# A fused attention and expert layer on one core: stores of one group on ScalarE's queue, three TensorE modes in the planner, new planning numbers

## The chip, the cores and the metric

The program runs on one core of a Trainium2 chip. The time is the device time of one execution in microseconds (us). A core has engines that run side by side: TensorE (PE; its weight loads, PEld, are shown apart), VectorE (DVE), ScalarE (ACT), GpSimd (POOL), and SyncE (SP), which here only issues DMAs. ScalarE can issue DMAs too. Each engine works through its own instructions in the order in which the program holds them and waits at an instruction until the semaphores that it names are reached.

## The reference

Causal attention over 4 batches of 12 heads (448 positions, 64 wide), then a two-layer block over all 1,792 tokens, all in float32.

```python
scores = scale * np.matmul(q, k.transpose(0, 1, 3, 2))
scores = np.where(mask, -1000000000.0, scores)
scores = scores - np.max(scores, axis=-1, keepdims=True)
attn = np.exp(scores)
attn = attn / (np.sum(attn, axis=-1, keepdims=True) + 1e-09)
attn_out = np.matmul(attn, v)
x = attn_out.transpose(0, 2, 1, 3).reshape(B * S, H * D)      # 1792 x 768
h = x @ w_in                                                  # 768 -> 2048
g = h * np.clip(h + 3.0, 0.0, 6.0) / 6.0
out = g @ w_out                                               # 2048 -> 768
```

## The kernel before

**What is computed where.** A *unit* is one pair of heads of one batch, 24 in all (`unit`, line 420). For each unit TensorE makes the scores (line 490: row tiles of 112 positions, the two heads side by side in 64 rows of the array each), VectorE adds the mask and takes the row's bound (line 505), ScalarE takes the exponential with the row sum (line 512), VectorE inverts the sums (lines 522 and 523), one of GpSimd, ScalarE or VectorE scales the rows (line 531 on ScalarE, line 533 on the others), TensorE transposes the rows in 112 x 112 blocks (line 553), ScalarE or VectorE copies them out of PSUM (lines 361 and 364), and TensorE multiplies with V (line 566: 112 rows, the two heads in 64 columns of the array each). The first six units score in plain float32; the later ones in three products of split numbers.

**The two layers.** A float32 matrix product is made as three products of operands that are split into a high and a low part (`triple`, lines 640 to 642): 696 triples of 128 x 128 by 128 x 448, 2,088 products. A *group* is one batch. Group 0 goes through `first_layer(0)` and `early_products`, group 1 through `first_layer(1)` and `middle`, groups 2 and 3 together through `last_first` and `last_second`, which save products by sums and differences of blocks. The weights come as 64-bit words and are turned into float32 by VectorE (`words`, lines 603, 605 and 608); they are kept in DRAM (`kept_w`, `kept_s`) and read again. The first layer's outputs of group 0 are kept in DRAM too (`kept_g`, line 686), for `middle`, which works with groups 0 and 1 together.

**What sets the order.** Nothing in the program runs in the order in which it is written. Every step is an `Op` with a key (a due time, made from `T_FIRST`, `T_PACE`, `UNIT`, `LOADS`, `WORDS`, the `K_...` numbers and so on), with the engines that may do it, and how much later than the first of them each may take it (`A_LAG`, `NORM_LAG`, `A_FIRST`). `Flow.run` plays the program through once at build time: whenever an engine is free, it takes from the ready steps the one with the lowest key whose buffers are free, and the resulting list of instructions is what the chip gets. `BUFS`, `BANKS` and `MOST` say how many buffers of each kind there are. Two rules are TensorE's alone. It has a mode: *tiled* for scores and products with V, not tiled for transposes and the layers' products; a step of the same mode is preferred until another's key is earlier by `KEEP` of the mode, and a change of mode costs time in the plan:

```python
                        if e != "PE" or o.tiled == self.mode:
                            chosen = o, need
                            break
                        if not chosen:
                            chosen, limit = (o, need), o.key[0] + self.KEEP[self.mode]
```

And where the plan finds TensorE idle between 20 and 36 us, `fill` puts in matmuls that compute nothing used (line 1072), so that the array stays at work. Ahead of the first scores stand four products of the tile `warm`, which compute nothing used either (line 1092).

DMAs stand in one queue, SyncE's, in the plan's order; three stand in ScalarE's: the first unit's two loads of k, and one of the last stores. A load or store is issued by `dma` (line 348), which has an argument for the queue; the framework gives the DMAs eight semaphores in turn, and an issue waits until the DMA that last used its semaphore has landed.

In the rows below, `gh` and `gl` are the large buffers that first hold q, k and v of batch 0, `d` is the pool of general buffers, `b` a PSUM bank, `wd` the weights as loaded, `wh` and `wl` their high and low parts, `prow` the row statistics, `r` a 128 x 448 scratch buffer.

Of the kernel before, what the change touches and what calls it, by code (L numbers as in the profile page):

```python
# [17 lines left out]
B, H, S, D = 4, 12, 448, 64  # L18
DM, DFF = 768, 2048
C = 112  # L20
# [10 lines left out]

T_FIRST = -113
T_PACE = 4
T_EARLY = 8
T_EACH = 11
T_LATE = 74
T_DENSE = 7.25
T_LOAD = -8
T_W = 10
T_WLOAD = 9  # L40
T_XA = 166
T_X = 175
T_LAST = 182
T_PAIR = 10.5
T_SECOND = T_LAST + 8 * T_PAIR
T_SECOND_GROUP = 72
T_MID = 120
T_BACK = 40
T_WORDS = 77
M_LOAD = 20  # L50
E_WORDS = 6.5
K_SCORES = 0
K_TURN = 6.5
K_TURNS = 0.6
K_PRODUCT = 14
K_GATE = 5
KEEP_FULL = 0
KEEP_TILED = 6.5
N_RAW = 6
DEPTH = 3  # L60
A_FIRST = 4
D_FIRST = 0.4
T_V = 11
FINE = 3
W_FROM = 3
W_BEHIND = 4
UNIT = [-80, -17, 5, 2.5, 0.5, -1, -2, -1.5, 5.5, 0.5, -6.5, -3, -3.5, -8, -2.5, -4.5, -1, -1.5, -6, -4.5, -2.5, 1, -4, 3]
LOADS = [-70, -38, -8, 10, 0, -10, 12, -14, -22, -4, -20, -14, 10, 4, -12, 2, -8, -12, -2, -28, -10, -4, 4, -6]
K_KEEP = -4
K_G = 4  # L70
GATE_FROM = 1
WORDS = [1, 8, -6, 4, -3, 7, -5, 0, -4, 3, -6, 0, 6, -2, 7, -4, 2, 4, 2, 3, -2, 2, -8, -4, 8, 3, -7, 5]
T_ISSUE = 0.36
NORM_LAG = 1.5
A_LAG = 0

# [8 lines left out]
    ps="b s most ps", tp="b s most", av="b s", mo="b mo", c="b c",  # L85
)
MOST = dict(qk=3, op=4, wf=4, sf=6, x=8, pt=6, pr3=4, pr20=5, xq=6, xc=21, gt=12, gm=9, so=3, s=8, most=8, ps=8, mo=2, c=8)

# [22 lines left out]
class Flow:  # L111
# [5 lines left out]
    BEGIN, LATENCY = 0.8, 0.12  # L117
    SWITCH = 0.4
    TAIL = dict(PE=.1, D=.085, A=.105, P=.04, SP=0)

    KEEP = KEEP_FULL, KEEP_TILED
    QUEUE, WARM = 8, 4
    DMA_PACKET, DMA_RATE, DMA_LANES, DMA_LATENCY = 0.008, 23e3, 16, 2.1
# [8 lines left out]

    def op(self, key, ways, parts, r=(), tiled=False, nbytes=0):

        w = [x for _, _, ws in parts for x in ws]
        bufs = {x[0] for x in list(r) + w if isinstance(x[0], Buf)}
        o = Op((key, len(self.ops)), ways, parts, bufs, nbytes)
        o.tiled = tiled
        for b in bufs:
            b.refs += 1  # L140
        before = {}
        for x in list(r) + w:
            if x in self.wrote:
                a, i = self.wrote[x]
                before[a] = max(before.get(a, 0), i)
        for x in w:
            for a in self.readers.pop(x, ()):
                before[a] = len(a.parts) - 1
        for x in r:
            self.readers.setdefault(x, []).append(o)  # L150
        for i, (_, _, ws) in enumerate(parts):
            for x in ws:
                self.wrote[x] = o, i
        before.pop(o, None)
        for a, i in before.items():
            a.then.append((o, i))
        o.waits = len(before)
        self.ops.append(o)
        return o

    def run(self):
# [3 lines left out]
        busy = dict.fromkeys(lists, self.BEGIN)  # L165
        self.dma, self.mode, self.port, tick = 0.0, False, 0.0, 0
        left = len(self.ops)
# [97 lines left out]
    def start(self, o, e, now, need, out, busy, post):  # L265
# [5 lines left out]
        if e == "PE" and o.tiled != self.mode:  # L271
            t += self.SWITCH / 2
            self.mode = o.tiled
# [28 lines left out]
def tile_causal_attention_hardswish_moe(ctx: ExitStack, tc: tile.TileContext, q, k, v, w_in, w_out, out):  # L302
    nc = tc.nc
# [40 lines left out]

    def pe(key, parts, r, tiled=False):
# [74 lines left out]
    def unit(b, p):  # L420
# [70 lines left out]

        cost, more = (1.667e-3, .06) if raw32 else (1.25e-3, .08)
        for a, two in enumerate(((1, 0), (3, 2)) if at == 0 else ((3, 2), (1, 0))):
# [3 lines left out]
                [(cost * C * (i + 1) + more, lambda i=i: products(i), [(ps[e, i][0], i) for e in range(2)] + [("turn",)]) for i in two],  # L497
                (halves_[0] if at == a == 0 else reads) + [("unit", at - (2 if b else DEPTH))], True,
            )
# [42 lines left out]
        for e in range(2):  # L542
            for js, ph in zip(GROUPS, pairs):
# [10 lines left out]

                pe(key, [(.096 * len(blocks) + .03, turn, [(tp, 0)])], [pk[e, i] for i in sorted({i for i, _ in blocks})])
                move(
# [13 lines left out]

        pe(t + K_PRODUCT, [(10 * C * 1.667e-3, times_v, [(av, 0), (av, 1), ("unit", at)])], deps, True)
        if b < 2:
# [73 lines left out]
    def first_layer(g):  # L646
# [5 lines left out]
        for i in range(NF):  # L652
# [32 lines left out]
            )  # L685
            dma(t + .5 + K_G, 4 * S, lambda i=i: kept_g[i], lambda r=r: ap(r), [(r, 0)], [("g", i)])
            move(t, S, lambda i=i: ap(gh)[:, i], lambda r=r: ap(r), [(r, 0)], [(gh, i)], {"A": 1})
# [403 lines left out]
    for _ in range(Flow.WARM):  # L1091
        nc.tensor.matmul(ap(b)[:C, :C], warm, warm, start=True, stop=True)

# [48 lines left out]
```

## Time and profile before

| | |
|---|---|
| three runs | 583.20, 583.35, 584.42 us; median 583.35 us |
| the profiled execution | 583.93 us, its span 582.2 us |
| TensorE busy | 573.8 us, 99% of the span |
| VectorE busy | 486.7 us, 84% |
| ScalarE busy | 405.7 us, 70% |
| GpSimd busy | 233.4 us, 40% |
| TensorE in the chain that ended last | 88% |

The span runs from the first to the last instruction of the one execution that was profiled; the 1.7 us between it and that execution's time lie around it. A timeline row has the start, the duration, the engine, the line, the operation, and in brackets the idle time ahead of it with what ended it. TensorE's float32 matmuls have two records each, and the records' ends are modelled and overlap; so the distance from start to start tells the cost, not the duration. The three layers' products are one every 0.20 us.

### The profile page before, as it was taken

The numbers are of one execution on the slowest core, as the hardware profiler recorded it, in microseconds if no ns is written. First come the engines' busy times: TensorE is split into PE (matmuls) and PEld (weight loads), VectorE is DVE, ScalarE is ACT, GpSimd is POOL, SyncE is SP. The second block draws the span as 40 slices with busy tenths as digits, with TensorE's granted clock in tenths as the row PEclk, the third lists the DMA queues.
The fourth block names the chain that finished last, engine by engine and source line by source line (L and its number), as shares of the span: only waits on it lengthen the run. The fifth ranks groups of instructions, "written<-read, shape, count | busy, mean of one in ns | idle before, by whom it ended". The sixth has DMA issues, their size and how long they took to land.

```text
span 582.2 us, 10686 instructions
## 1 busy us (share of the span) xinstructions
PE 573.8 (99%) x3496; PEld 502.5 (86%) x3496; DVE 486.7 (84%) x1093; ACT 405.7 (70%) x973; POOL 233.4 (40%) x226
## 2 busy tenths in 40 slices
PE   8999999999999999999999999999999999999997
PEld 5667988988888788888988989899999999999996
DVE  5899999899689787999998668999888799985652
ACT  6997885888757666899988968576555586454530
POOL 2678889874447344776274212034000042100000
PEclk9999999999999999999999999999999999999999
DMA  8958999967579898999832254441211424443411
GB/s 235 334 184 278 315 319 362 395 230 233 179 267 303 258 385 267 329 381 304 301 114 76 94 165 145 160 128 56 82 55 55 128 64 135 133 133 111 138 64 48
DMA packets 61352, 115.59 MB, mean 199 GB/s; under 512 B 6512, under 2 KB 36592, under 8 KB 61296
## 3 DMA queue, kind: packets, MB, share of 16 engines
q1 hardware_dynamic: 60576, 114.34, 59.5%
q10 hardware_dynamic: 720, 0.57, 0.3%
q8 instruction: 27, 0.44, 0.3%
q14 instruction: 29, 0.24, 0.1%
HBM read 83.39 MB, written 31.49 MB: 197 GB/s over the span
## 4 chain that ended last, share of the span: by engine, by line
PE 88%; DMA 5%; DVE 3%; ACT 2%; issue 1%; SPq 0%; DVEq 0%; ACTq 0%
PE b L640 24%; PE b L641 23%; PE b L642 23%; PE b L566 7%; PE b L553 6%; PE b L490 5%; DMA gl<-in_v_dram 2%; DMA wd<-in_w_in_dram 1%; DMA wd<-in_w_out_dram 1%; ACT d L512 1%; DVE b L603 1%; DVE d L608 1%; DVE b L505 1%; DVE b L605 1%; ACT gl L512 0%
## 5 line engine op out<-in xcount | busy, mean ns | idle before, releaser
L640 PE MATMUL b<-d,wh 128*128 128x448 f32 x624 | 231.4, 371 | 0.7 <-ACT d L512 0.7
L641 PE MATMUL b<-d,wh 128*128 128x448 f32 x624 | 226.3, 363 | 0.0
L642 PE MATMUL b<-d,wl 128*128 128x448 f32 x624 | 225.7, 362 | 0.0
L640 PEld LDWEIGHTS b<-d,wh 128*128 128x128 f32 x624 | 117.2, 188 | 10.6 <-ACT d L512 1.2
L642 PEld LDWEIGHTS b<-d,wl 128*128 128x128 f32 x624 | 116.9, 187 | 9.0 <-POOL wl L373 0.4
L641 PEld LDWEIGHTS b<-d,wh 128*128 128x128 f32 x624 | 117.2, 188 | 6.3
L361 ACT CAST wh<-wd 128x768 fp32r<-128x768 f32 x88 | 73.6, 836 | 70.1 <-PE b L641 61.5
L373 DVE TENSOR_TENSOR wl<-wd,wh 128x768 fp32r<-128x768 f32 x74 | 79.7, 1077 | 26.0 <-ACT wh L361 25.0
L505 DVE CUSTOM_DVE_ANT_0 b<-b,mask 112x224 f32<-112x224 f32 (+1 forms) x192 | 80.2, 479 | 19.6 <-PE b L490 17.2
L512 ACT ACTIVATE d<-b,prow 112x448 f32<-112x448 f32 (+2 forms) x144 | 72.2, 517 | 15.5 <-DVE prow L505 13.1
L373 POOL TENSOR_TENSOR d<-d 128x896 fp32r<-128x896 f32 (+3 forms) x28 | 43.2, 1548 | 36.3 <-DVE d L373 23.4
L553 PE MATMUL b<-ident,d 112*112 112x112 f32 x384 | 55.9, 261 | 1.2 <-ACT d L512 0.8
L373 POOL TENSOR_TENSOR wl<-d,wh 128x768 fp32r<-128x768 f32 (+1 forms) x28 | 46.1, 1649 | 23.9 <-ACT wh L361 14.9
L361 ACT COPY d<-b 112x336 f32<-112x336 f32 (+1 forms) x104 | 43.7, 494 | 7.5 <-PE b L553 6.9
L553 PEld LDWEIGHTS b<-ident,d 112*112 112x112 f32 x384 | 42.7, 133 | 5.6 <-POOL gl L533 1.0
L533 POOL TENSOR_SCALAR d<-d,prow 112x112 f32<-112x112 f32 (+2 forms) x59 | 29.4, 509 | 31.7 <-DVE prow L523 25.4
L566 PE MATMUL b<-d,vr 112*64 112x224 f32 (+3 forms) x288 | 37.5, 405 | 0.0
L531 ACT ACTIVATE d<-d,prow 112x336 f32<-112x336 f32 (+2 forms) x66 | 33.8, 548 | 4.2 <-DVE prow L523 4.2
L603 DVE TENSOR_SCALAR b<-wd 128x384 int32<-128x384 int32 (+1 forms) x56 | 32.9, 613 | 3.0 <-DMA wd<-in_w_out_dram 2.5
L490 PE MATMUL b<-d 64*112 64x448 f32 (+3 forms) x432 | 35.0, 305 | 0.0
L490 PEld LDWEIGHTS b<-d 64*112 64x112 f32 x432 | 30.2, 172 | 5.5 <-issue 1.2
L566 PEld LDWEIGHTS b<-d,vr 112*64 112x64 f32 x288 | 19.1, 136 | 18.4 <-issue 10.7
(111 smaller groups left out, 934.3 us busy)
## 6 DMA issues: line engine op xcount, KB each, us to landing
wd<-in_w_in_dram SPq DMA_DIRECT2D x32, 384.0 KB, 6.0
wd<-in_w_out_dram SPq DMA_DIRECT2D x24, 512.0 KB, 6.6
wd<-kept_w SPq DMA_DIRECT2D x32, 384.0 KB, 4.7
wd<-kept_s SPq DMA_DIRECT2D x32, 384.0 KB, 3.0
kept_w<-d SPq DMA_DIRECT2D x16, 384.0 KB, 6.2
kept_w<-d SPq DMA_DIRECT2D x24, 256.0 KB, 5.4
kept_s<-d SPq DMA_DIRECT2D x24, 256.0 KB, 3.8
wd<-kept_w SPq DMA_DIRECT2D x48, 128.0 KB, 2.2
```

The lines of the kernel that those rows point to most:

```text
L361: nc.scalar.copy(o(), i()) if scale is None else nc.scalar.mul(o(), i(), scale)
L373: (nc.gpsimd if e == "P" else nc.vector).tensor_tensor(o(), a(), b(), op)
L490: nc.tensor.matmul(score(e, i), qx[m, c], kx[m, :w], start=n == 0, stop=n == len(terms) - 1)
L505: lambda _, e=e, i=i, w=w: nc.vector.tensor_tensor_reduce(score(e, i), score(e, i), mask[:, S - w:], -0.125, 3.0e38, ALU.add, ALU.min, ap( ...
L512: lambda _, e=e, i=i: nc.scalar.activation(row_of(pr, e, i), score(e, i), ACTF.Exp, bias=ap(st)[:, e, i:i + 1], scale=-1.0, accum_out=ap(s ...
L531: nc.scalar.mul(x, x, ap(st)[:, e, 4 + i:5 + i])
L553: nc.tensor.transpose(ap(tp)[:C, C * n:C * n + C], row_of(pr, e, i)[:, C * j:C * j + C], ident)
L566: nc.tensor.matmul(ap(av)[64 * e:64 * e + 64, S - w:S], va()[:, j, e, :], ap(ph)[:, e, o:o + w], start=(j == 0), stop=(j == NC_ - 1),)
L603: nc.vector.tensor_scalar(ti, high, 3, 0x3FFFFFFF, ALU.logical_shift_left, ALU.bitwise_and)
L640: nc.tensor.matmul(ps, ap(wh)[:, a], xh, start=start, stop=False, skip_group_check=more)
L641: nc.tensor.matmul(ps, ap(wh)[:, a], xl, start=False, stop=False, skip_group_check=more)
L642: nc.tensor.matmul(ps, ap(wl)[:, a], xh, start=False, stop=stop, skip_group_check=more)
```

## The change

One argument sends the sixteen stores of `kept_g` through ScalarE's queue. The planner gets three modes of TensorE in place of two: 0 for transposes and the layers' products, 1 for scores, 2 for products with V; a change between any two costs 0.1 in the plan where a change cost 0.2 (`SWITCH / 2`), and a score, a product with V and a transpose block are priced a little differently. `KEEP_TILED`, how long a tiled mode is held against an earlier key, goes from 6.5 to 2.5. The four products of `warm` become eleven of half the columns. And nearly all numbers that make the keys are others. The diff, with the number tables cut to one line:

```diff
-T_FIRST = -113
-T_PACE = 4
+T_FIRST = -73
+T_PACE = 12.5
...
-KEEP_TILED = 6.5
+KEEP_TILED = 2.5
...
-A_FIRST = 4
-D_FIRST = 0.4
+A_FIRST = 5.2
+D_FIRST = 0
...
-UNIT = [-80, -17, 5, 2.5, 0.5, -1, -2, -1.5, 5.5, 0.5, -6.5, -3, -3.5, -8, -2.5, -4.5, -1, -1.5, -6, -4.5, -2.5, 1, -4, 3]
+UNIT = [-86, 0, 5, -3, -8, -1.5, -8, 7.5, 8, 2.5, -5, -6, -5, -8, -0.5, -6.5, 0, -5.5, -7, -6, -1, 4.5, -1.5, 2]
...
-NORM_LAG = 1.5
-A_LAG = 0
+NORM_LAG = 0.75
+A_LAG = 3.2
...
-    SWITCH = 0.4
+    SWITCH = 0.1
...
-    KEEP = KEEP_FULL, KEEP_TILED
-    QUEUE, WARM = 8, 4
+    KEEP = KEEP_FULL, KEEP_TILED, KEEP_TILED
+    QUEUE, WARM = 8, 11
...
         if e == "PE" and o.tiled != self.mode:
-            t += self.SWITCH / 2
+            t += self.SWITCH
             self.mode = o.tiled
...
-        pe(t + K_PRODUCT, [(10 * C * 1.667e-3, times_v, [(av, 0), (av, 1), ("unit", at)])], deps, True)
+        pe(t + K_PRODUCT, [(10 * C * 1.667e-3 + .07, times_v, [(av, 0), (av, 1), ("unit", at)])], deps, 2)
...
-            dma(t + .5 + K_G, 4 * S, lambda i=i: kept_g[i], lambda r=r: ap(r), [(r, 0)], [("g", i)])
+            dma(t + .5 + K_G, 4 * S, lambda i=i: kept_g[i], lambda r=r: ap(r), [(r, 0)], [("g", i)], "A")
...
-        nc.tensor.matmul(ap(b)[:C, :C], warm, warm, start=True, stop=True)
+        nc.tensor.matmul(ap(b)[:C, :C // 2], warm, warm[:, :C // 2], start=True, stop=True)
```

What this does to the order is shown at three places. On TensorE, in the head, behind the second unit's transposes: L553 is a block of transposes, L1072 the idle filler, L490 scores of the fourth unit.

```order
 L553 MATMUL b<-ident,gl 112x112
 L553 MATMUL b<-ident,d 112x112 x5
-L1072 MATMUL b<-identr 112x112 x4
 L490 MATMUL b<-gh 112x448 x2
 L490 MATMUL b<-gh 112x336 x2
```

The filler is gone here and at its one other place; nothing else is put there.

On TensorE, where the first long run of products of the first layer begins. Before, two units' products with V, then the whole of the next unit's scores, then 63 products:

```order
L566 MATMUL b<-d,gl 64x224 x2
L566 MATMUL b<-d,gl 64x112 x2
L490 MATMUL b<-d 112x448 x6
L490 MATMUL b<-d 112x336 x6
L490 MATMUL b<-d 112x224 x6
L490 MATMUL b<-d 112x112 x6
L640 MATMUL b<-d,wh 128x448
```

Now:

```order
L490 MATMUL b<-d 112x448 x6
L490 MATMUL b<-d 112x336 x6
L566 MATMUL b<-d,gl 64x448 x2
L566 MATMUL b<-d,gl 64x336 x2
L566 MATMUL b<-d,gl 64x224 x2
L566 MATMUL b<-d,gl 64x112 x2
L640 MATMUL b<-d,wh 128x448
L641 MATMUL b<-d,wh 128x448
L642 MATMUL b<-d,wl 128x448
L490 MATMUL b<-d 112x224 x6
L490 MATMUL b<-d 112x112 x6
```

The scores are cut in two; the first half stands ahead of the products with V, and three products of the layer stand between it and the second half, behind which the 63 follow.

On VectorE, in the head, behind the third unit's sums (L522 and L523), with L603, L605 and L608 the conversion of the first weights and L505 the next unit's scores. Before:

```order
L522 TENSOR_SCALAR b<-prow 112x8
L523 RECIPROCAL prow<-b 112x2x4
L603 TENSOR_SCALAR b<-wd 128x384 x2
L605 SCALAR_TENSOR_TENSOR b<-wd,b 128x384 x2
L608 SCALAR_TENSOR_TENSOR d<-wd,b 128x384 x2
L505 ISA b,prow<-b,mask 112x448
```

Now:

```order
L505 ISA b,prow<-b,mask 112x336
L505 ISA prow 112x1
L603 TENSOR_SCALAR b<-wd 128x384 x2
L605 SCALAR_TENSOR_TENSOR b<-wd,b 128x384 x2
L608 SCALAR_TENSOR_TENSOR d<-wd,b 128x384 x2
L505 ISA b,prow<-b,mask 112x224
```

The six conversions, which stood ahead of all eight of that unit's score rows, stand behind the first four of them.

## Rows read from the trace of the kernel before

**Rows 1.** Busy time by stretch: the head, and two of 40 us
```profile
core 0: us, PE busy (x) PEld busy (x) DVE busy (x) ACT busy (x) POOL busy (x), PEclk, DMA share, GB/s
0.00:53.40 53.40, 49.08 (x361) 33.52 (x361) 43.83 (x162) 43.15 (x140) 33.11 (x58) 1.00 0.82 253
...
60.00:100.00 40.00, 40.00 (x241) 35.30 (x241) 38.81 (x94) 30.38 (x67) 35.23 (x29) 1.00 0.96 330
100.00:140.00 40.00, 40.00 (x275) 35.60 (x271) 34.74 (x92) 34.48 (x95) 29.53 (x26) 1.00 0.83 295
```

**Rows 2.** Timeline of TensorE in the head
```profile
1.08 1.83 PE L1092 MATMUL b<-warm 64*112 64x112 f32 x8 [1.08 <-DVE warm L385]
3.58 4.08 PE L490 MATMUL b<-gh 64*112 64x224 f32 x16 [0.67 <-DMA gh<-in_k_dram]
8.42 5.96 PE L490 MATMUL b<-gh 64*112 64x448 f32 x32 [0.76 <-DMA gh<-in_k_dram]
...
21.98 0.60 PE L1072 MATMUL b<-identr 112*112 112x112 f32 x4
...
29.88 2.15 PE L490 MATMUL b<-gh 64*112 64x448 f32 x16
...
47.69 3.99 PE L566 MATMUL b<-d,gl 112*64 112x448 f32 x32 [0.17 <-DVE d L608]
51.62 1.87 PE L490 MATMUL b<-d 64*112 64x448 f32 x24
53.41 0.48 PE L640 MATMUL b<-d,wh 128*128 128x448 f32 x1
```

**Rows 3.** Timeline of ScalarE in the head, one row
```profile
24.91 0.63 ACT L512 ACTIVATE d<-b,prow 112x448 f32<-112x448 f32 x1 [1.19 <-DVE prow L505]
```

**Rows 4.** Timeline of VectorE in the head, two rows
```profile
21.88 0.54 DVE L603 TENSOR_SCALAR b<-wd 128x384 int32<-128x384 int32 x1
...
52.61 0.63 DVE L505 CUSTOM_DVE_ANT_0 b<-b,mask 112x448 f32<-112x448 f32 x1 [1.29 <-PE b L490]
```

**Rows 5.** Timeline of TensorE: products with V, then scores, between layer products
```profile
98.40 0.37 PE L642 MATMUL b<-d,wl 128*128 128x448 f32 x1
98.70 2.11 PE L566 MATMUL b<-d,vr 112*64 112x448 f32 x16
100.74 1.89 PE L490 MATMUL b<-d 64*112 64x448 f32 x24
...
103.07 0.37 PE L642 MATMUL b<-d,wl 128*128 128x448 f32 x1
```

**Rows 6.** The same around scores alone
```profile
114.47 0.37 PE L642 MATMUL b<-d,wl 128*128 128x448 f32 x1
...
117.11 0.37 PE L642 MATMUL b<-d,wl 128*128 128x448 f32 x1
```

**Rows 7.** The same around products with V alone
```profile
363.83 0.37 PE L642 MATMUL b<-d,wl 128*128 128x448 f32 x1
...
366.68 0.36 PE L642 MATMUL b<-d,wl 128*128 128x448 f32 x1
```

**Rows 8.** The same around four transposes
```profile
66.30 0.26 PE L553 MATMUL b<-ident,d 112*112 112x112 f32 x1
66.40 0.26 PE L553 MATMUL b<-ident,pr 112*112 112x112 f32 x1
...
67.11 0.37 PE L642 MATMUL b<-d,wl 128*128 128x448 f32 x1
```

**Rows 9.** Waits of TensorE behind 53 us: us in total, times, longest
```profile
PE b L640 <- ACT d L512: 0.7, 1, 0.7
```

**Rows 10.** Waits of SyncE's queue from 53 to 140 us, same columns
```profile
SPq L352 <- DVE r L683: 9.2, 7, 5.7
...
SPq L352 <- DMA wd<-in_w_out_dram: 4.5, 6, 1.1
```

**Rows 11.** All instructions on `kept_g`: ns least, median, most
```profile
L352 SPq DMA_DIRECT2D kept_g<-r x16: 320/327/501, 59.0 to 129.6; - x16
```

**Rows 12.** Scaling of rows on VectorE by form: count, busy us, mean ns
```profile
L533 DVE TENSOR_SCALAR d<-d,prow 112x448 f32<-112x448 f32 x9 | 4.0, 442 | 0.0
```

More of the change, by code (lines that the diff above doesn't have):

```diff
@@ L37 @@
 T_DENSE = 7.25
-T_LOAD = -8
+T_LOAD = -12
 T_W = 10
 T_WLOAD = 9
-T_XA = 166
-T_X = 175
+T_XA = 156
+T_X = 172
 T_LAST = 182
 T_PAIR = 10.5
-T_SECOND = T_LAST + 8 * T_PAIR
+T_SECOND = 266
 T_SECOND_GROUP = 72
@@ L49 @@
 T_WORDS = 77
-M_LOAD = 20
+M_LOAD = 12
 E_WORDS = 6.5
 K_SCORES = 0
-K_TURN = 6.5
+K_TURN = 6
 K_TURNS = 0.6
-K_PRODUCT = 14
-K_GATE = 5
+K_PRODUCT = 11.5
+K_GATE = 1
 KEEP_FULL = 0
-KEEP_TILED = 6.5
+KEEP_TILED = 2.5
 N_RAW = 6
 DEPTH = 3
-A_FIRST = 4
-D_FIRST = 0.4
-T_V = 11
+A_FIRST = 5.2
+D_FIRST = 0
+T_V = 3
 FINE = 3
@@ L66 @@
 W_BEHIND = 4
-UNIT = [-80, -17, 5, 2.5, 0.5, -1, -2, -1.5, 5.5, 0.5, -6.5, -3, -3.5, -8, -2.5, -4.5, -1, -1.5, -6, -4.5, -2.5, 1, -4, 3]
-LOADS = [-70, -38, -8, 10, 0, -10, 12, -14, -22, -4, -20, -14, 10, 4, -12, 2, -8, -12, -2, -28, -10, -4, 4, -6]
-K_KEEP = -4
-K_G = 4
+UNIT = [-86, 0, 5, -3, -8, -1.5, -8, 7.5, 8, 2.5, -5, -6, -5, -8, -0.5, -6.5, 0, -5.5, -7, -6, -1, 4.5, -1.5, 2]
+LOADS = [4, -24, -40, -22, 12, -14, -18, 12, 0, -20, -2, 8, -12, 4, -20, -24, 0, -12, 2, -8, -18, -8, -2, -22]
+K_KEEP = -6
+K_G = 6
 GATE_FROM = 1
-WORDS = [1, 8, -6, 4, -3, 7, -5, 0, -4, 3, -6, 0, 6, -2, 7, -4, 2, 4, 2, 3, -2, 2, -8, -4, 8, 3, -7, 5]
+WORDS = [-1, 8, 4, 7, -5, 4, 3, 7, 8, 7, -5, -6, -7, -4, 7, -1, 3, -8, -4, 5, 4, -3, -8, 2, -2, 5, -7, -8]
 T_ISSUE = 0.36
-NORM_LAG = 1.5
-A_LAG = 0
+NORM_LAG = 0.75
+A_LAG = 3.2
 BUFS = dict(
@@ L86 @@
 )
-MOST = dict(qk=3, op=4, wf=4, sf=6, x=8, pt=6, pr3=4, pr20=5, xq=6, xc=21, gt=12, gm=9, so=3, s=8, most=8, ps=8, mo=2, c=8)
+MOST = dict(qk=3, op=4, wf=5, sf=8, x=8, pt=8, pr3=3, pr20=2, xq=6, xc=21, gt=12, gm=7, so=3, s=8, most=8, ps=8, mo=4, c=8)
 ORDERED = dict(sf=3, wd=0, wh=1, wl=2, xq=3, xc=3, gt=3, gm=3, pr3=4, pr2=5, pr1=6, pr20=9, pt=7, op=8)
@@ L131, in __init__, with op @@
         self.ops, self.wrote, self.readers, self.landed = [], {}, {}, []
-    def op(self, key, ways, parts, r=(), tiled=False, nbytes=0):
+    def op(self, key, ways, parts, r=(), tiled=0, nbytes=0):
         w = [x for _, _, ws in parts for x in ws]
         bufs = {x[0] for x in list(r) + w if isinstance(x[0], Buf)}
-        o = Op((key, len(self.ops)), ways, parts, bufs, nbytes)
+        o = Op((round(key, 5), len(self.ops)), ways, parts, bufs, nbytes)
         o.tiled = tiled
@@ L165, in run @@
         busy = dict.fromkeys(lists, self.BEGIN)
-        self.dma, self.mode, self.port, tick = 0.0, False, 0.0, 0
+        self.dma, self.mode, self.port, tick = 0.0, 0, 0.0, 0
         left = len(self.ops)
@@ L343, in one, with pe @@
             o.port = set()
-    def pe(key, parts, r, tiled=False):
+    def pe(key, parts, r, tiled=0):
         flow.op(key, {"PE": (1, 0)}, [(d, lambda e, g=g: g(), w) for d, g, w in parts], r, tiled)
@@ L490, in products @@
                     nc.tensor.matmul(score(e, i), qx[m, c], kx[m, :w], start=n == 0, stop=n == len(terms) - 1)
-        cost, more = (1.667e-3, .06) if raw32 else (1.25e-3, .08)
+        cost, more = (1.667e-3, .06) if raw32 else (1.25e-3, .09)
         for a, two in enumerate(((1, 0), (3, 2)) if at == 0 else ((3, 2), (1, 0))):
@@ L497, in unit @@
                 [(cost * C * (i + 1) + more, lambda i=i: products(i), [(ps[e, i][0], i) for e in range(2)] + [("turn",)]) for i in two],
-                (halves_[0] if at == a == 0 else reads) + [("unit", at - (2 if b else DEPTH))], True,
+                (halves_[0] if at == a == 0 else reads) + [("unit", at - (2 if b else DEPTH))], 1,
             )
@@ L553, in turn @@
                         nc.tensor.transpose(ap(tp)[:C, C * n:C * n + C], row_of(pr, e, i)[:, C * j:C * j + C], ident)
-                pe(key, [(.096 * len(blocks) + .03, turn, [(tp, 0)])], [pk[e, i] for i in sorted({i for i, _ in blocks})])
+                pe(key, [(.096 * len(blocks), turn, [(tp, 0)])], [pk[e, i] for i in sorted({i for i, _ in blocks})])
                 move(
```

## The prediction

> **What bounds the kernel now.** I read the busy times first: TensorE is at work 99% of the span and makes 88% of the chain that ended last. So nothing counts but what TensorE does between its products, and when it stands still. The windows say where that is: from 60 to 140 us it is busy 80.00 of 80 us, in the first 53.4 us only 49.08 [rows 1], and of those 53.4 a part was spent at the low clock. Behind 53 us the waits of TensorE hold one entry, 0.7 us [rows 9]. The matmuls are the same before and after but for filler, so the new time is the old one plus three differences: the cost of changing between kinds of matmul, the moment at which the long run of layer products begins (53.41 us [rows 2]) with what has been done by then, and the waits behind it.
>
> **What a change of kind costs.** Starts tell it. A product follows a product in 0.20 us. From the last product ahead of a unit's products with V and another's scores to the third product behind them are 4.67 us; less three products, 4.07 [rows 5]. Scores alone take 2.64 less 0.60, so 2.04 [rows 6]; products with V alone 2.85 less 0.60, so 2.25 [rows 7]. Apart they cost 4.29, side by side 4.07: 0.22 is saved by standing together. Two units' products with V take 3.93 from start to start [rows 2], one takes 2.04 [rows 5], so a unit itself costs 1.89, and going in and out costs 2.25 - 1.89 = 0.36, or 0.18 a change; between V and scores it is then 0.36 - 0.22 = 0.14. I take 0.17 for a change into or out of either. Four transposes cost hardly more than themselves: 0.81 us from their first to the third product behind them, less two products and four times 0.10, leaves 0.01 [rows 8].
>
> Counted in the two orders of TensorE, changes between transposes and products fall from 99 to 69, worth nothing by these rows (at the most a few tenths of a us). Changes with scores or products with V on one side rise from 72 to 89: between them and the rest from 50 to 78, between the two from 22 to 11. The new plan charges 0.1 for any change and holds a mode less long, and so it pulls V and scores apart. Seventeen more at 0.17 are 2.9 us; by the ends of the price, 28 at 0.18 less 11 at 0.14 are 3.5 and 17 at 0.14 are 2.4. Five of the seventeen lie ahead of the long run, twelve (2.0 us) behind it.
>
> **The head.** There the other engines bound: VectorE was busy 43.83 and ScalarE 43.15 of 53.4 us [rows 1]. I listed what each must have done before the long run can begin, in either order. VectorE gives up two scalings of rows and takes three copies out of PSUM; a scaling is 0.44 or less [rows 12], and a copy is of about that size too, so I put 0.7 us more on it. ScalarE has one scaling and three copies less and one conversion exchanged, some 1.6 us less. Beside the sums two waits go. The weights' conversion stood ahead of scores on VectorE from 21.88 on, and ScalarE waited 1.19 us for those scores [rows 3, 4]; now scores stand first. And VectorE waited 1.29 us for the scores behind two units' products with V [rows 4]; half of these scores now come first. If VectorE sets the moment, it moves between +0.7 (its sum, no wait saved) and -0.6 (1.29 saved). I take the middle, no shift. But by then six products more have been done (15 in place of 9 ahead of the run), 1.2 us of TensorE's time. The filler that goes (0.60 us at each of two places [rows 2]) and the five changes of kind lie in time that TensorE has to spare there, so they are in this range and not extra.
>
> **The clock.** [...] Eleven products of half the columns are 37% more columns than four whole ones, so the warm-up lasts some 2.5 us and the first gap shrinks to little. If the clock rises sooner, the second and third units' scores shorten by up to 0.8 us each, of which the engines behind them, busy without a break, can pass on one: 0 to 0.8 us, and I take 0.2, since the load that ends the second gap is as late as before. [...]
>
> **The stores.** Sixteen issues of some 0.33 us leave SyncE [rows 11], which had waited 9.2 us in seven cases for the data of these stores with loads behind them [rows 10]. TensorE waited for none of those loads, so I count no gain. ScalarE gets 16 x 0.33 = 5.3 us of issue between 59 and 130 us, where it idles 15.1 of 80 [rows 1], and is rid of 57 scalings over the whole program (92 to 35). No row shows a store on ScalarE; the price is between nothing and the rival below, and I take nothing, because sum and idle time fit.
>
> **Behind the run.** Twelve changes cost 2.0, six products need not be done again, -1.2: +0.8. VectorE takes most of ScalarE's scalings (24 to 60 on VectorE, 76 to 97 on GpSimd): 36 at up to 0.44 [rows 12] are at most 16 us over the span, and it idled 95. The 0.7 us wait [rows 9] stood behind weights that landed late; the same loads are there, so I leave it, and add nothing.
>
> **The sum.** 0 for the head, -0.2 for the clock, +0.8 behind: +0.6 us, and -0.1 for the changes with transposes: +0.5. The profiled execution's 583.93 us becomes 584.4. It lies 0.58 above the median of its kind, so against the median 583.35 I predict 583.8. About 0.2%, 1.2 us, is what a measurement can tell from no change, and this is inside it.
>
> **Rivals.** *The head pays out.* Against my sum, the run starts 0.6 us earlier, the clock gives its other 0.6, the 0.7 wait and as much again of short ones vanish: 583.8 - 0.6 - 0.6 - 1.3 = 581.3. For it: the conversions and half the scores are placed just where waits of 1.19 and 1.29 stood, and the filler is gone. Against it: TensorE pays its changes whatever the head does.
>
> *VectorE takes over as the bound*, on the slow side. From 60 to 100 us it is busy 38.81 of 40, 97%, and TensorE does not wait; from 100 to 140 it idles 5.3 [rows 1]. In the first 400 layer products the new order asks it for some 5 us more. That leaves 1.5 of 6.5 us idle, 98%, more than any row shows. Where it needs 5% of idle time, 4 us, TensorE stands for 2.5, and what the head may have gained is lost with it: 583.8 + 2.5 = 586.3; it decides as soon as VectorE cannot stay above 97% there, and at 97% it is 0.9, so 584.7.
>
> *The stores block ScalarE.* Each waits for the DMA that used its semaphore before; SyncE's waits of this sort came to 1.1 us at the longest [rows 10]. Sixteen such, 17.6 us, with 5.3 of issue, exceed the 15.1 of idle time by 8; if a quarter of that reaches the weights' high parts, which ScalarE makes, it is 2 us: 585.8. [...] Against it: the stores stand behind the conversion of the same data, so they wait for no data.
>
> *The change does not do what it says*: the new price of a change of kind, 0.1, is below the 0.14 to 0.18 of the rows, so the plan spends more than it knows; that is in the sum.
>
> **How the numbers follow.** Forecast, within 0.2%: 0.41. The head pays out, faster: 0.27. VectorE, 0.20, and the stores, 0.12, slower: 0.32 together. The forecast's own range, from the price of the changes (-0.4 to +0.4 on the twelve), the head (-0.6 to +0.7) and the clock (-0.6 to +0.2), is 582.4 to 584.9. To hold 8 in 10 it reaches to the rivals: 581.3 to 586.2.
>
> **What would show it.** Apart, scores and products with V must again cost 2.04 and 2.25 us with 89 changes in the records; the long run begins between 52.8 and 54.1 us; TensorE's waits behind it stay near 1 us; VectorE's busy time rises to about 500 us and ScalarE's falls. It is wrong if the run begins before 52.5 us, if the clock row or the scores at 8.4 us show the full rate early, if changes cost less where they stand now, or if TensorE's waits name VectorE's scalings or ScalarE's conversions for more than 1.5 us.

## The result and the profile after

The changed kernel takes 588.25 us, the median of 4 runs (587.73 to 588.41), against 583.28 before; the ratio is 1.0079, with a 95% interval of 1.0061 to 1.0097. Beside another set of runs it was 1.0080 (1.0065 to 1.0094). So it is slower by 4.6 to 5.0 us. The prediction was 583.8 with a range to 586.2, and it was wrong.

The profiled execution takes 588.27 us with a span of 586.5, 4.3 more than before. I read it in the order of the prediction. First the stretches, as in [rows 1]:

```profile
core 0: us, PE busy (x) PEld busy (x) DVE busy (x) ACT busy (x) POOL busy (x), PEclk, DMA share, GB/s
0.00:53.40 53.40, 51.03 (x363) 36.09 (x363) 44.69 (x163) 40.60 (x134) 35.83 (x62) 1.00 0.85 255
60.00:100.00 40.00, 40.00 (x230) 36.06 (x230) 34.66 (x80) 25.77 (x56) 34.25 (x30) 1.00 0.97 355
100.00:140.00 40.00, 37.88 (x266) 31.42 (x265) 37.76 (x101) 31.17 (x87) 31.10 (x34) 1.00 0.87 294
```

TensorE, which was busy 40.00 of 40 us from 100 to 140 us, now lacks 2.1 us there. VectorE had less done from 60 to 100 us (34.66 in place of 38.81) and more from 100 to 140 (37.76 in place of 34.74): part of its work came later. It was not overloaded first.

Then TensorE's timeline, as in [rows 2]: the warm-up, the first scores, and the start of the long run.

```profile
1.08 4.16 PE L1092 MATMUL b<-warm 64*112 64x56 f32 x21 [1.08 <-DVE warm L385]
4.86 0.71 PE L490 MATMUL b<-gh 64*112 64x224 f32 x1
...
54.10 0.47 PE L640 MATMUL b<-d,wh 128*128 128x448 f32 x1
```

The warm-up lasts 4.16 us (21 of its 22 records; the last one stands at 5.04), not 1.83, and the first scores start at 4.86 in place of 3.58. The long run starts 0.69 us later than before, although six more products and five more changes of kind lie ahead of it. And TensorE's waits behind 53 us, one entry of 0.7 in [rows 9], are now these (us in total, times, longest):

```profile
PE b L553 <- POOL d L533: 1.3, 2, 0.9
PE b L553 <- DVE d L608: 0.5, 1, 0.5
PE b L553 <- ACT d L512: 0.4, 1, 0.4
PE b L553 <- DVE d L364: 0.2, 1, 0.2
```

That is the account of the 4.3 us: 0.7 at the start of the long run, and 3.6 behind it (586.5 less 54.10 is 532.4; before, 582.2 less 53.41 is 528.8). Of the 3.6 the prediction has 0.8, for twelve changes of kind less the six products done early, and the rows of waits name 1.7 more (2.4 less 0.7). The last 1.1 are in no row.

SyncE got rid of most of its waits for the stores' data, 9.2 us in [rows 10], as the change meant, though its waits for converted weights (`d` of line 608) grew from 23.0 to 34.4 us in the same stretch:

```profile
SPq L352 <- DVE r L683: 1.2, 2, 0.6
```

But look at ScalarE's timeline ahead of 100 us, where it issues two of these stores between two conversions of weights:

```profile
86.69 0.84 ACT L361 CAST wh<-d 128x768 fp32r<-128x768 f32 x1
88.52 1.27 ACTq L352 DMA_DIRECT2D kept_g<-r  x2
89.89 0.84 ACT L361 CAST wh<-d 128x768 fp32r<-128x768 f32 x1 [2.36 <-PE b L490]
90.63 0.63 ACT L669 ACTIVATE r<-b,three 128x448 f32<-128x448 f32 x1
```

The first conversion ends at 87.53. Two issues of 0.33 us should let the next one start at 88.2; it starts at 89.89. The bracket blames TensorE's scores. That is an inference of the profile, and experiment 6 shows that it is wrong: it is the stores that waited. The data of both had been written by VectorE by 85.8 us. Each also waits for the DMA that used its semaphore last. The trace's semaphore records have these land at 88.50 us (a store of `kept_w`) and at 89.44 (a load of `wd`), and the two stores go out at 88.52 and 89.47. Four more of the sixteen go out within 0.03 us of such a landing in this trace, at 74.13, 82.44, 109.43 and 113.25.

### The profile page after: what moved, and what is told of

It is laid out like the page before. It is cut to its first block, busy times and chain, and to the rows that moved or that the text cites. A ratio compares the mean times of both kernels' runs of the same rounds, so it can differ in the third digit from the quotient of the medians.

```text
span 586.5 us, 10687 instructions
## 1 busy us (share of the span) xinstructions
PE 578.5 (99%) x3502; PEld 503.9 (86%) x3502; DVE 495.3 (84%) x1128; ACT 385.2 (66%) x920; POOL 232.5 (40%) x244
## 4 chain that ended last, share of the span: by engine, by line
PE 83%; DVE 5%; DMA 4%; ACT 1%; issue 1%; DVEq 0%; SPq 0%
PE b L640 23%; PE b L641 22%; PE b L642 21%; PE b L566 7%; PE b L553 6%; PE b L490 5%; DMA wd<-in_w_out_dram 2%; DMA kept_w<-d 1%; DVE b L605 1%; DVE b L603 1%; DVE d L608 1%; DMA d<-in_k_dram 1%; DVE b L505 1%; DVE d L364 0%; DVE r L683 0%
## 5 line engine op out<-in xcount | busy, mean ns | idle before, releaser
L373 DVE TENSOR_TENSOR wl<-wd,wh 128x768 fp32r<-128x768 f32 x73 | 77.0, 1055 | 25.1 <-ACT wh L361 24.2
L505 DVE CUSTOM_DVE_ANT_0 b<-b,mask 112x224 f32<-112x224 f32 (+1 forms) x192 | 80.0, 481 | 18.6 <-PE b L490 16.6
L553 PE MATMUL b<-ident,d 112*112 112x112 f32 x384 | 54.6, 261 | 2.8 <-POOL d L533 1.3
L373 POOL TENSOR_TENSOR wl<-d,wh 128x768 fp32r<-128x768 f32 (+1 forms) x27 | 44.0, 1640 | 24.0 <-ACT wh L361 10.7
L533 POOL TENSOR_SCALAR d<-d,prow 112x112 f32<-112x112 f32 (+2 forms) x73 | 35.6, 501 | 32.4 <-ACT d L512 14.4
L553 PEld LDWEIGHTS b<-ident,d 112*112 112x112 f32 x384 | 42.2, 133 | 7.2 <-POOL d L533 2.3
L373 DVE TENSOR_TENSOR d<-d 128x512 f32<-128x512 f32 (+3 forms) x55 | 41.7, 775 | 2.7 <-DMA kept_w<-d 1.6
L373 POOL TENSOR_TENSOR wl<-wd,wh 128x768 fp32r<-128x768 f32 x15 | 27.8, 1853 | 29.4 <-ACT wh L361 20.9
L490 PEld LDWEIGHTS b<-d 64*112 64x112 f32 x432 | 30.2, 172 | 6.7 <-issue 1.8
L373 POOL TENSOR_TENSOR d<-gh,d 128x448 fp32r<-128x448 f32 x9 | 10.3, 1154 | 62.4 <-DVE gh L373 55.6
L490 PE MATMUL b<-d 64*112 64x448 f32 (+3 forms) x432 | 35.0, 305 | 0.0
```

The costliest lines, as they stand in the source:

```text
L373: (nc.gpsimd if e == "P" else nc.vector).tensor_tensor(o(), a(), b(), op)
L490: nc.tensor.matmul(score(e, i), qx[m, c], kx[m, :w], start=n == 0, stop=n == len(terms) - 1)
L505: lambda _, e=e, i=i, w=w: nc.vector.tensor_tensor_reduce(score(e, i), score(e, i), mask[:, S - w:], -0.125, 3.0e38, ALU.add, ALU.min, ap( ...
L533: (nc.gpsimd if w == "P" else nc.vector).tensor_scalar(x, x, ap(st)[:, e, 4 + i:5 + i], 1.0, ALU.mult, ALU.mult)
L553: nc.tensor.transpose(ap(tp)[:C, C * n:C * n + C], row_of(pr, e, i)[:, C * j:C * j + C], ident)
```

## The experiments

Theory P, held at first: the loss is the seventeen more changes of kind and new waits of TensorE behind the run, and the head gains. Rival W: the warm-up holds up the head. Rival S: the stores block ScalarE. Numbers in brackets behind a ratio are its 95% interval.

| run | us | ratio to before | long run starts | from there to the end |
|---|---|---|---|---|
| the kernel before | 583.28 | 1 | 53.41 | 528.8 |
| the changed kernel | 588.25 | 1.0079 [1.0061, 1.0097] | 54.10 | 532.4 |
| the changed kernel, again | 587.56 | 1.0080 [1.0065, 1.0094] | 54.08 | 531.7 |
| with the old warm-up | 586.30 | 1.0040 [1.0027, 1.0052] | 52.81 | 531.9 |
| with the stores on SyncE | 586.01 | 1.0040 [1.0024, 1.0055] | 54.14 | 530.4 |
| with two stores on SyncE | 586.51 | 1.0059 [1.0046, 1.0072] | 54.08 | 530.4 |
| with old warm-up and stores on SyncE | 584.29 | 1.0012 [0.9996, 1.0027] | 52.46 | 530.1 |
| before, with the new warm-up | 585.38 | 1.0025 [1.0012, 1.0038] | 54.04 | 528.7 |

The last two columns, in us, are of the one profiled execution of each. In the changed kernel the warm-up moves the first of them and the stores move the second.

**1. The changed kernel with the old warm-up.**

```diff
-    for _ in range(Flow.WARM):
-        nc.tensor.matmul(ap(b)[:C, :C // 2], warm, warm[:, :C // 2], start=True, stop=True)
+    for _ in range(4):
+        nc.tensor.matmul(ap(b)[:C, :C], warm, warm, start=True, stop=True)
```

> The changed kernel with the old warm-up, four products of 112 columns in place of eleven of 56; every other instruction and every order stays. Theory P (price): the 4.9 us come from what lies behind 54 us, three of it the seventeen more changes of kind and three the new waits of TensorE, and the head gives 1.7 back. Then the warm-up has no large part: the first scores move from 4.86 back to about 3.6 us, the clock rises later (12 us in place of 8.5), and the two about cancel: 587.6 to 588.9 us. Rival W (warm-up): eleven short products take as long each as whole ones and hold the first scores up by 1.3 us, and all of the head behind them: 586.9 us or less. The opposite end: the later clock costs the second and third unit up to 0.8 us each, and the time is 589 to 590 us.

Measured: 586.30 us. The excess over before falls from 0.0080 to 0.0040, 2.3 us. Rival W is confirmed, and theory P's claim that the warm-up has no large part falls. TensorE's timeline, first and at the start of the long run:

```profile
1.08 1.83 PE L1092 MATMUL b<-warm 64*112 64x112 f32 x8 [1.08 <-DVE warm L385]
3.53 2.21 PE L490 MATMUL b<-gh 64*112 64x224 f32 x10 [0.62 <-DMA gh<-in_k_dram]
...
52.81 0.47 PE L640 MATMUL b<-d,wh 128*128 128x448 f32 x1
```

The scores start 1.33 us earlier, and the long run 1.29: nearly all of the delay had passed through the head. The weight loads of the two warm-ups (count, busy us, mean ns) help to say why it was so long; of the changed kernel, up to 4.8 us:

```profile
L1092 PEld LDWEIGHTS b<-warm 64*112 64x112 f32 x21 | 4.0, 301 | 1.1 <-DVE warm L385 1.1
```

and of this run, with whole products:

```profile
L1092 PEld LDWEIGHTS b<-warm 64*112 64x112 f32 x8 | 1.6, 298 | 1.1 <-DVE warm L385 1.1
```

A float32 product is two passes here (eight records for four products), and from the second on the passes follow each other at 0.19 us whether 56 or 112 columns move. Each loads 112 columns of weights in 0.30 us in either case. Halving the columns that move saved nothing, and eleven products are 22 passes. No run here has another number of weight columns in the warm-up, so what sets the time of a pass is not shown.

**2. The kernel of before with the new warm-up** (the same edit the other way round).

> The kernel of before with the new warm-up alone, eleven products of 56 columns in place of four of 112. Theory P: no more than 0.7 us either way, 582.6 to 584.0 us, with the clock up some 3 us earlier and the first scores 1.3 us later. Rival W: the first scores' delay passes on, +1.3 us, 584.6 us. A gain of more than 0.7 us would say that the earlier clock is worth more than the delay.

Measured: 585.38, a ratio of 1.0025 [1.0012, 1.0038]: 0.7 to 2.2 us slower. The warm-up costs by itself, without the new order. As for the clock, a trace's record of the granted clock opens with 1.0, the full rate, at the moment of the rise (the printed PEclk column counts the time ahead of it as full). That it is a rise, the scores' passes with 448 moving columns tell: before, a pair of them follows a pair in 0.75 us at 4.84 us, and in 0.38 at 12.21, with the record's first entry at 12.15. It rises at 10.19 us in this trace and at 8.49 in the changed kernel, in both behind a warm-up and scores that leave TensorE no idle time, and at 12.15 in that of before, which has idle times of 0.67 and 0.76 us [rows 2]. But with the old warm-up it rises at 8.77 in experiment 1, 6.80 in 5 and 7.62 in 10, where one idle time of 0.62 to 0.66 us stands ahead of the scores and none behind: an early rise didn't need the longer warm-up.

**3. The changed kernel with the stores on SyncE**, the plan as it is.

```diff
-        start = nc.sync.dma_start if queue == "SP" else nc.scalar.dma_start
+        start = nc.sync.dma_start if queue == "SP" or sync else nc.scalar.dma_start
...
-            dma(t + .5 + K_G, 4 * S, lambda i=i: kept_g[i], lambda r=r: ap(r), [(r, 0)], [("g", i)], "A")
+            dma(t + .5 + K_G, 4 * S, lambda i=i: kept_g[i], lambda r=r: ap(r), [(r, 0)], [("g", i)], "A", sync=True)
```

> The changed kernel with the sixteen stores of the first layer's outputs issued by SyncE again, at the places in time at which the plan had put them on ScalarE; TensorE, VectorE, GpSimd and the rest of ScalarE stand in the order of the changed kernel. Theory P: the stores cost ScalarE 5.3 us of issue that lies in its idle time, and no wait: 587.6 to 588.9 us. Rival S (the stores block ScalarE): its waits behind 54 us, the 3.1 us, go: 585.2 us, or 586.5 where half of them go. Slower than 589 us would say that loads behind the stores on SyncE's queue are held, and that the move to ScalarE was worth something.

Measured: 586.01 us. The excess falls by 0.0040 again. Rival S is confirmed too, with about the size that it had in the prediction, 2 us, though the quarter in that sum was a guess. ScalarE's timeline at the same place, without the stores:

```profile
86.72 0.84 ACT L361 CAST wh<-d 128x768 fp32r<-128x768 f32 x1
87.93 0.84 ACT L361 CAST wh<-d 128x768 fp32r<-128x768 f32 x1 [0.37 <-PE b L641]
88.67 0.63 ACT L669 ACTIVATE r<-b,three 128x448 f32<-128x448 f32 x1
```

The second conversion starts 1.96 us earlier, and the activation behind it as well. How that came to TensorE can be followed engine by engine, in the order of each engine's instructions. In the changed kernel VectorE takes up that activation's result late, and the reciprocal of the unit's sums stands behind it and behind the conversion of weight words:

```profile
91.29 0.62 DVE L683 SCALAR_TENSOR_TENSOR r<-r,b 128x448 f32<-128x448 f32 x1 [1.18 <-ACT r L669]
...
100.10 0.21 DVE L523 RECIPROCAL prow<-b 112x8 f32<-112x8 f32 x1
```

GpSimd scales one row, then has two low parts in its order, then the other three rows:

```profile
100.48 0.36 POOL L533 TENSOR_SCALAR d<-d,prow 112x112 f32<-112x112 f32 x1 [0.58 <-DVE prow L523]
...
103.77 1.42 POOL L533 TENSOR_SCALAR d<-d,prow 112x336 f32<-112x336 f32 x3
```

and TensorE's transposes of these rows wait twice:

```profile
104.39 0.41 PE L553 MATMUL b<-ident,d 112*112 112x112 f32 x2 [0.95 <-POOL d L533]
...
105.85 0.28 PE L553 MATMUL b<-ident,d 112*112 112x112 f32 x1 [0.48 <-DVE d L608]
```

With the stores on SyncE the reciprocal comes at 98.84:

```profile
98.84 0.21 DVE L523 RECIPROCAL prow<-b 112x8 f32<-112x8 f32 x1
```

and the first wait is gone, the second shorter (of all the waits behind 53 us, 2.4 us, the three that experiment 5 shows are left, 0.8):

```profile
103.31 0.35 PE L553 MATMUL b<-ident,d 112*112 112x112 f32 x2
...
104.59 0.28 PE L553 MATMUL b<-ident,d 112*112 112x112 f32 x1 [0.36 <-DVE d L608]
```

The move had little to save for TensorE: sixteen issues of 0.33 us left SyncE, and no row of TensorE's waits behind 53 us names a DMA, before or after. On ScalarE the pair at 88.52 us cost more than its two issues of 0.33 us, since it waited in the queue: the 1.96 us above.

**4. The changed kernel again**, beside the next two.

> The changed kernel itself, unedited, on the chip and beside the runs of the next two, so that the edits can be set against it and not only against the kernel before: 587.5 to 588.8 us by every theory, with ScalarE's conversion of weights at about 90 us again some 2 us behind the one before it.

Measured: 587.56 (587.16 to 588.33). In this execution the two stores go out at 87.92 in place of 88.52, and TensorE waits 0.6 for GpSimd in place of 1.3. The earlier transfers land at 87.90 and 88.80 here: in these two traces what the pair costs goes with their landing.

**5. The changed kernel with both edits.**

> The changed kernel with both edits at once: the old warm-up and all sixteen stores on SyncE. The first alone gave 586.3, the second 586.0, against 588.25. If the two are separate losses (theory WS: warm-up 1.9 us, a store that holds ScalarE 2.2 us, and changes of kind that the better head pays for), the time is 583.6 to 584.8 us, that of the kernel before or a little above. If either only made room that the other also makes, it stays at 585.5 us or more, and the changes of kind (3.0 us) are then the rest. Below 582.5 us would say that changes of kind cost next to nothing.

Measured: 584.29 (584.11 to 584.39), 1.0012 of before [0.9996, 1.0027]. Of an excess of 0.0080 either edit alone took 0.0040 and both take 0.0068: the two losses are separate and add up but for a rest inside the intervals, and what is left of the change can't be told from no change. In the profiled execution that rest is a run that starts 0.95 us earlier than before and needs 1.3 us longer behind its start, where the prediction had 0 and 0.8. Timeline of TensorE:

```profile
3.57 2.21 PE L490 MATMUL b<-gh 64*112 64x224 f32 x10 [0.66 <-DMA gh<-in_k_dram]
...
52.46 0.47 PE L640 MATMUL b<-d,wh 128*128 128x448 f32 x1
```

and its waits behind 53 us:

```profile
PE b L553 <- DVE d L608: 0.4, 1, 0.4
PE b L553 <- DVE d L364: 0.2, 1, 0.2
PE b L553 <- ACT d L512: 0.2, 1, 0.2
```

**6. Only two stores on SyncE**, those at 88.52 us (`sync=i in (6, 7)` in the edit of experiment 3).

> The changed kernel with two of the sixteen stores on SyncE, those that ScalarE issued at 88.52 us between two conversions of weights; the other fourteen stay on ScalarE. If the loss is the wait of this pair on ScalarE's queue (2 us, behind which the weights' conversion, then GpSimd's low part, then VectorE's reciprocal come late, until TensorE's transposes wait at 104 us), the two give nearly all of what sixteen gave: 586.0 to 586.6 us. If the sixteen issues of 0.33 us each load ScalarE evenly, two give an eighth of 2.2 us: 587.9 us or more.

Measured: 586.51, 1.05 less than experiment 4 beside it, and each of its runs (586.11 to 586.99) lies below each of that one's (587.16 to 588.33). An even load would have given an eighth of 2.2 us, so the pair costs far more than its share. How much of the sixteen it is stays open: half by the ratios (0.0021 of 0.0040, from runs on two chips, with wide intervals), and all by the profiled executions, which need 530.4 us behind the start of the run with two stores moved as with sixteen. The conversion is back in its place with no other instruction moved, which settles that the stores held it:

```profile
86.66 0.83 ACT L361 CAST wh<-d 128x768 fp32r<-128x768 f32 x1
87.86 0.83 ACT L361 CAST wh<-d 128x768 fp32r<-128x768 f32 x1 [0.37 <-PE b L641]
```

**7, 8 and 9. The price of a change of kind.** One more matmul ahead of the first product of each of 32 blocks, in the kernel of before; `rows, cols` is `C, C` in 7, `64, C` in 8 and `C, 64` in 9.

```diff
                 def products(cs=cs, wh=wh, wl=wl, acc=acc):
+                    if 0 in cs:
+                        nc.tensor.matmul(ap(acc)[:cols, :C], identr[:rows, :cols], identr[:rows], start=True, stop=True)
                     for c in cs:
```

> The kernel of before with one more matmul ahead of the first product of each of the 32 blocks of a first layer (16 in each of two groups), into the bank that this product then starts anew: 112 rows of weights by 112 columns over all rows, of the kind of the products themselves. It is the reference for the next two: a quarter of a product's 448 columns, so some 0.05 us each, 1.6 us in all, 585 us.

> The same 32 extra matmuls, but with 64 rows in place of 112, the kind of the scores: TensorE changes kind on either side of each. By the price read from starts, 0.16 to 0.18 us a change, 64 changes cost 10.2 to 11.5 us against the run with the same matmul of the products' kind: 595 to 597 us, and 0.32 to 0.36 us more from the last product ahead to the third behind. By the price that the changed plan charges, 0.1, it is 6.4 us: 591.5 us. If changes of kind are hidden by the loading of weights, it is nothing: 585 us.

> The same again with 112 rows of weights and 64 columns of them, so that 64 rows of the output are written, the kind of the products with V. By the price read from starts (0.18 us into or out of V) 64 changes cost 11.5 us against the run with the full kind: 597 us. If only the rows that a matmul reads make its kind, and not those that it writes, this costs nothing: 585 us.

Measured: 585.56, 593.73 and 585.50 us. Timelines of 7 and 8, from the last product ahead to the second behind:

```profile
82.31 0.36 PE L642 MATMUL b<-d,wl 128*128 128x448 f32 x1
82.52 0.21 PE L662 MATMUL b<-identr 112*112 112x112 f32 x1
82.57 0.42 PE L640 MATMUL b<-d,wh 128*128 128x448 f32 x1
82.83 0.36 PE L641 MATMUL b<-d,wh 128*128 128x448 f32 x1
```

```profile
82.17 0.37 PE L642 MATMUL b<-d,wl 128*128 128x448 f32 x1
82.47 0.30 PE L662 MATMUL b<-identr 64*112 64x112 f32 x1
82.70 0.47 PE L640 MATMUL b<-d,wh 128*128 128x448 f32 x1
83.01 0.37 PE L641 MATMUL b<-d,wh 128*128 128x448 f32 x1
```

0.52 us becomes 0.84: two changes cost 0.32, so 0.16 each, where the prediction took 0.17. So it is at 26 of the 32 places, behind products and behind transposes. Behind a product with V it is 0.13, and at five places behind scores, whose kind the extra matmul has, nothing: 26 x 0.32 and 0.13 are 8.4, and 8.2 were measured. So theory P's price stands for these places, and the changed plan's 0.1 is too low. Experiment 9 was a surprise: one matmul with 64 columns of weights into the first 64 rows is no change of kind (0.52 us at the same place).

**10. The kernel of before with its first loads in another order.**

```diff
+    sp = [n for n, x in enumerate(order) if x[2] == "SP"]
+    early = [order[sp[n]] for n in (0, 1, 3, 4, 6, 7, 2, 5)]
+    for n, x in enumerate(early):
+        order[sp[n]] = x
```

> The kernel of before with the first loads of SyncE in another order: the queries and keys of the second and third pair of heads ahead of the values of the first and second. In the profiled execution TensorE waited 0.76 us at 7.66 us for the second pair's keys, and the first transposes began at 15.19 us; in the changed kernel, with the old warm-up, there is no such wait, and they begin at 14.1. If this order of loads is what the changed kernel's head gains by, the long run begins up to 1 us earlier and the time is 582.2 to 583.2 us; if VectorE and ScalarE bound the head whatever the loads do, it is 583.3 to 583.9 us.

Measured: 583.38, a ratio of 0.9999 [0.9989, 1.0009]. In its profiled execution TensorE doesn't wait at 7.66 us, the first transposes begin at 14.11 and the long run starts at 52.45; in the median there is no gain. The wait itself is not one execution's luck: the traces of experiments 7, 8, 9 and 12, which have the loads of before, show it too, between 0.34 us (7) and 0.97 (12). TensorE's scores in 7, in 12 and here:

```profile
7.75 5.50 PE L490 MATMUL b<-gh 64*112 64x448 f32 x32 [0.34 <-DMA gh<-in_k_dram]
```

```profile
8.56 6.21 PE L490 MATMUL b<-gh 64*112 64x448 f32 x32 [0.97 <-DMA gh<-in_k_dram]
```

```profile
3.56 9.92 PE L490 MATMUL b<-gh 64*112 64x224 f32 x48 [0.64 <-DMA gh<-in_k_dram]
```

What varies is its length, and with it the head: in the five traces with the loads of before the first transposes begin between 13.88 and 15.32 us (15.19 in the one from which I counted). Why the median of this run gains nothing although the wait is gone in its trace stays open.

**11. Experiment 5 with eight blocks of products moved on TensorE.** `lined` is TensorE's part of the order; the pairs name entries of it.

```diff
+    lined = [x for x in order if x[2] == "PE"]
+    for a, b in [(134, 128), (264, 262), (191, 187), (210, 209), (288, 287), (328, 323), (169, 167), (234, 233)]:
+        order.remove(lined[a])
+        order.insert(order.index(lined[b]), lined[a])
```

> The changed kernel with the old warm-up and the stores on SyncE (584.29 us as it stands), and with eight of the 363 blocks of products moved on TensorE by one or two places; nothing moves on another engine. Five of them stood alone between a unit's products with V and scores (or between two halves of scores) and now stand ahead, so that TensorE changes kind twelve times less; three stood behind transposes for which TensorE waited in the trace, and now stand ahead of them. Theory P (a change of kind costs 0.14 to 0.18 us wherever it stands behind the head, and the waits at 102, 133 and 186 us are of the transposes alone): four places give 0.18 to 0.20 each, the halves of scores 0.32, the waits up to 1.3 us: 582.2 to 583.2 us, at or below the kernel before. If other engines set the pace there, what TensorE saves comes back as waits at the next transposes: 584 us or more.

Measured: 585.55 us, slower than experiment 5 by 1.26. (The expectation miscounts: there are ten changes less with products, four more between V and scores, so six less in all, 1.0 us.) The waits of TensorE behind 53 us:

```profile
PE b L553 <- DVE d L364: 0.6, 1, 0.6
PE b L640 <- ACT d L512: 0.5, 1, 0.5
PE b L490 <- ACT r L361: 0.4, 1, 0.4
...
```

With two more of 0.2 these are 1.9 us in place of 0.8, all for engines whose own order had not changed. So some of the time that changes should have saved came back as waits. But had the full 1.0 been saved, 2.3 us would have to come back, and the rows name 1.1: the rest stays open, and so does whether the price of a change holds at these places. It is no version that beats the kernel before, and none was found.

**12. A pair built like the products with V**: the edit of 7 to 9 with two float32 matmuls, `for e in range(2)`, from `ident[:C, :64]` into rows `64 * e` to `64 * e + 64`.

> The kernel of before with a pair of extra matmuls ahead of the first product of each of the 32 blocks of a first layer, built as the last pair of a unit's products with V is: float32, 112 rows of 64 weight columns by 112 columns, one into rows 0 to 63 and one into rows 64 to 127 of the bank. A single one into rows 0 to 63, not in float32, cost no more than a matmul of the products' own kind (585.5 against 585.56 us). If the 0.18 us into or out of V is a change of kind that the second half of the rows brings, each place costs 0.36 us beside the pair's own time (about 0.1 to 0.2 us, from the 1.89 us of a unit's eight by their columns): 585.5 + 32 x 0.36 = 597 us or more. If it is not a change but the length of the products with V themselves, there is only the pair's own time: 585 to 589 us, and 0.1 to 0.2 us more between the neighbours' starts than with the single one.

Measured: 597.14 us. Its timeline at the same kind of place:

```profile
81.74 0.37 PE L642 MATMUL b<-d,wl 128*128 128x448 f32 x1
82.04 0.41 PE L663 MATMUL b<-ident 112*64 112x112 f32 x4
82.38 0.48 PE L640 MATMUL b<-d,wh 128*128 128x448 f32 x1
82.70 0.36 PE L641 MATMUL b<-d,wh 128*128 128x448 f32 x1
```

0.96 us in place of 0.52, with 0.30 ahead of the pair and 0.32 between the two products behind it, the gaps of experiment 8 (0.30 and 0.31). The pair's four passes start within 0.15 us; the other 0.29 are near the 0.32 of two changes. So a pair built like those with V pays for going in and out, as the prediction took it for V. Whether float32 or the second 64 rows makes it so, against experiment 9, stays open; [rows 8] have float32 transposes over all rows between products at no price.

## Why the prediction was wrong, point by point

**The price and the count of changes: right, as far as tested.** 0.17 a change was taken, 0.16 is measured on scores (experiment 8), and a little less on pairs like V's (12). Seventeen more are then 2.7 us against 2.9. That was measured on matmuls put into the kernel of before; in the changed kernel six changes less did not save their 1.0 us (11).

**The head: the step on the warm-up failed.** It reads "Eleven products of half the columns are 37% more columns than four whole ones, so the warm-up lasts some 2.5 us and the first gap shrinks to little". It lasted 4.16, and the first scores started at 4.86: the gap was not filled, it was overrun by 1.28 us. I went by columns that move, where [rows 2] had the time of a pass (1.83 us for eight, 0.23 each) and nothing showed that it goes by columns. Without that step the head looks as the rival "the head pays out" said: the long run starts at 52.46 to 52.81 in experiments 5 and 1, and the six products and five changes lie ahead of it. How much of that is the new order stays open, since the head of before varies by 1.4 us from trace to trace (experiment 10). With the step, the run started at 54.10, the end of the range that I gave (52.8 to 54.1): that it fell on the range is luck.

**The clock: wrong in cause, and its size not shown.** I gave -0.2 for a fuller warm-up, out of up to 0.8 us a unit, the 2.98 us of a unit's scores at 8.42 less the 2.15 at 29.88 [rows 2]. The clock did rise earlier, at 8.49 in place of 12.15 us, but it does so without the new warm-up where no load interrupts the scores (6.80 to 8.77 in experiments 5, 10 and 1). No run tells what the earlier rise was worth by itself, so none shows the 0.2 of the sum; what they show is the pace, 0.75 us for a pair of the scores' passes ahead of the rise and 0.38 behind it, in the trace of before.

**The stores: the price of nothing failed.** "I take nothing, because sum and idle time fit" counted issue time against idle time. What counted was the wait in front of an issue, and what stood behind it in the same queue. The rival had that mechanism and put 2 us on it; by the ratios it is 2.3 (experiment 3 against 4) and 1.6 (5 against 1). My reason against it, that the stores stand behind the conversion of the same data, was true and beside the point: the data was there, the semaphore was not. And what waits in ScalarE's queue held what stands behind it: the trace shows it from 88.52 us on, where the second store went out at 89.47 and the conversion behind it, which could have started at 88.2, at 89.89. The planner could not see it either: it counts a wait for earlier DMAs for SyncE alone (`if e == "SP"` in `start`).

**Behind the run: "I leave it, and add nothing" failed.** The waits that the rows name grew from 0.7 to 2.4 us, and most of that goes with the stores: with them alone on SyncE 0.8 are left (experiment 3), and the time behind the start of the run falls from 532.4 to 530.4 us. Of the 1.6 that this is still above 528.8, the prediction had 0.8; the rest is in no row.

**VectorE as the bound: not what happened.** It was busy 34.66 of 40 us from 60 to 100, less than before, and 37.76, 94%, from 100 to 140, below the 97% that it had before. At the one place followed above, it passed on a delay that began on ScalarE.

**The sum.** 583.8, 1.5 to 2.3 for the warm-up (experiments 2 and 1) and 1.6 to 2.3 for the stores make 586.9 to 588.4, and 587.56 and 588.25 were measured. The rival of the stores had been priced well enough; the warm-up had no rival, since no term let it cost anything. And I held the rivals to exclude each other and ended the range near the largest. The two losses, on different engines in different stretches, added up here but for a rest: 0.0040 each, 0.0068 together. That the rest of the sum came out (584.29 in experiment 5, against 583.8) is in part luck: the head gave more than the 0 that I took, and the stretch behind cost more than 0.8.

## What to carry to other kernels

A DMA put on a compute engine's queue can cost that engine the wait for the landing of the DMA whose semaphore it takes, beside its 0.33 us of issue (here the conversion behind such a pair started 1.96 us later than without it); read what stands right behind it, and put it where nothing urgent does. Time a warm-up by passes (0.19 us each here, with 56 moving columns as with 112), and end it before the first load lands (here the first scores started 1.28 us later where it did not). Ask of each rival whether it can happen together with the others before setting the end of a range, and don't take one execution's head as the kernel's: with one order of loads the first transposes began anywhere from 13.88 to 15.32 us here.

## What the runs showed of the hardware

In the warm-ups, ahead of the rise of the clock, a float32 pass with 112 columns of weights took 0.19 us from start to start with 56 moving columns as with 112. A single matmul with 64 weight columns into the first 64 rows stood between products at no cost beyond that of one over all (585.50 against 585.56 us, 0.52 us at the place in both), while one over 64 rows, or a float32 pair over both halves of the output rows, cost 0.29 to 0.32 us to go in and out. Six of the sixteen stores on ScalarE's queue went out within 0.03 us of the landing of the DMA that had used their semaphore last. And the profile named TensorE as the releaser of a conversion (2.36 us) that had waited for two DMA issues ahead of it on its own queue.
